# Storing the attention output by head pair, and two loads and a memset moved in the written order

## The chip, the cores and the metric

The kernel runs on one core of one Trainium2 chip. The metric is device time in microseconds of one launch. The core has a matrix engine (TensorE: PE for matmuls, PEld for its weight loads), a vector engine (DVE), a scalar engine (ACT), GpSimd (POOL) and SyncE (SP). SP does no arithmetic here: its instructions wait on semaphores and issue DMAs, one after the other. An instruction that waits on SP holds back everything behind it on SP.

## The reference

Eight batches of eight heads go through block-causal attention (576 tokens, 64 numbers a head, blocks of 64 tokens). The heads of one batch laid side by side are x, 576 rows of 512 floats. Then, for each batch, a score per row is computed, the 128 rows of highest score are picked, and a two-layer network is applied to those rows alone; the other rows are the attention output as it is.

```
scores = (q @ k.T) / 8, masked so that block_i >= block_j
attn   = exp(scores - max) / (sum + 1e-9)
x      = attn @ v, heads side by side            # (8, 576, 512)
s      = x @ w_gate
top    = the 128 rows of highest s, per batch
out    = x
out[top] = x[top] + sigmoid(s[top]) * (relu(x[top] @ w1) @ w2)
```

## The kernel before

**Pairs and beats.** Attention works on pairs of heads: 8 batches of 4 pairs make 32 pairs, p = 0 to 31. What happens to a pair is a list of steps, `STEPS` (lines 52 to 101): each has a time in beats, relative to the beat p of its pair, and a name. The plan (lines 737 to 744) is all steps of all pairs, sorted by p plus that time, and the program is written out in that order. So the order in `STEPS`, modulo one beat, is the order of the instructions on every engine: matmuls for `scores` of pair p are written at the beginning of beat p, those of `times_v` of pair p at p + 2.6857, its `divide` at p + 2.8556. A step is delayed in the plan if what it needs has not been written yet (lines 764 to 783). Every engine runs its own instructions in that order; what it waits for is put in by semaphores on the data.

**What a pair does.** `load` (line 304) brings q and k of the pair, 576 KB in one DMA on SP, into one of three buffers `qk`. `shrink` (line 315) scales q on POOL. `scores` (line 355) is a set of matmuls. `maxima` (DVE) and `exps` (ACT) follow. `turn_p` and `keep_p` transpose the probabilities on PE and copy them out of PSUM. `load_v` (line 324) brings v in two DMAs on SP (264 KB and 99 KB) into one of three buffers `v`, and `ones` (line 332) writes a column of ones into it with one memset on POOL. `times_h` and `times_v` (lines 474 and 492) multiply by v. `invert` and `divide` (lines 510 and 515) divide by the sums and write the pair's 128 columns of `x_sb`, a tile for a whole batch (two of them).

**Which work frees a buffer.** `load` of pair p + 3 writes into the buffer that `scores` of pair p reads, `load_v` of pair p + 3 into the one that `times_v` of pair p reads. In `STEPS`, `load` stands at -2.75, that is 0.25 beats into the beat of the pair whose scores free it; these scores are written at 0.0 to 0.0448. `load_v` stands at 0.05; the `times_v` that frees its buffer stands 0.36 beats earlier (2.6857 - 3 = -0.3143).

**Stores.** At the last pair of a batch `divide` issues four DMAs on SP that store the batch's x (lines 525 to 532): 64 rows, 256 rows and twice 128 rows of 512 floats, 2 KB a row. They wait for the division, the DVE instruction of line 520. In the written order the next `load_v` comes behind them: 0.8556 of one beat against 0.05 of the next.

**Also in SP's queue.** The weights w1 and w2 come in 16 DMAs of 256 KB, behind `scores` of the pairs from the third on (`weights`, line 722). For six batches a row of scores goes out to DRAM and comes back spread over all partitions (`store` and `fetch`, lines 559 and 567). 

**Selection and experts.** When a batch's x is complete, `select` (line 536) makes the steps that rank its rows: five scores on DVE, comparisons on POOL (lines 608 to 620, for all but the last batch), counts by matmul, and row numbers (`idx_all`). They are strewn into later beats at the places that `STEPS` calls `vec`, `far`, `rank` and `spot`. The two-layer network (lines 1013 to 1087) runs behind attention, in two groups of four batches. It gathers its rows from the stored output by an indirect DMA on POOL (line 922), and its first part is begun in the last beats of attention.

Of the kernel before, what the change touches and what calls it, by code (L numbers as in the profile page):

```python
# [18 lines left out]
P = 128  # L19
# [10 lines left out]
PLACES = [1, 3, 0, 2, 4]  # L30
# [20 lines left out]

STEPS = [
    (-2.6704, 'far'),
    (-2.75, 'load'),
    (-0.95, 'shrink'),
    (0.0, 'scores', 2),
    (0.007, 'scores', 1),
# [22 lines left out]
    (0.9042, 'exps', 2),  # L80
    (0.9265, 'keep_p', (8, 7), 0),
    (0.9524, 'vec'),
    (0.05, 'load_v'),
    (0.9954, 'keep_p', (8, 7), 1),
    (1.0825, 'turn_p', (2, 1)),
    (1.108, 'turn_p', (6, 5)),
    (1.1476, 'turn_p', 'h'),
    (1.2343, 'turn_p', (4, 3)),
    (1.1, 'ones'),
    (1.6987, 'keep_p', (6, 5), 0),  # L90
    (1.6996, 'keep_p', (6, 5), 1),
    (1.8986, 'keep_p', (2, 1)),
# [56 lines left out]
def attention_topk_ffn(  # L149
# [11 lines left out]
    nc = tc.nc  # L161
    B, S, _ = out.shape
    H, D = 2 * qk.shape[1], qk.shape[2] // 2
# [33 lines left out]
    for x, r, base in ((0, slice(0, P), 0), (1, slice(0, 64), 64), (1, slice(64, P), 0)):  # L197
        nc.gpsimd.affine_select(
            out=later[x][r], in_=less_b[r], pattern=[[-1, P]], base=base, channel_multiplier=1, compare_op=ALU.is_ge, fill=0.0,
# [32 lines left out]
    def attention(att):  # L232
# [12 lines left out]
        def bank(p, use):  # L245

            return tuple(OTHER[x] for x in BANK[use]) if p % 2 else BANK[use]
# [9 lines left out]
        def give(p, use, part=None):  # L257
            for x in bank(p, use)[slice(None) if part is None else slice(part, part + 1)]:
                assert live[x][0:2] == [p, use], (p, use, live)
                live[x][2] -= 1  # L260
                if not live[x][2]:
                    live[x] = None
# [242 lines left out]
        def outcome(p):  # L505

            at = column(PLACES[0], 0)
            return st[p]["y"][:, at:at + 2 * (NT + 1) * WIDTH].rearrange("p (i h d) -> p i h d", h=2, d=WIDTH)
# [6 lines left out]
        def divide(p):  # L515
            b, h = pairs[p]
            if h == 0:
                xs[b] = xp.tile([P, NT + 1, DM], F32, name="x_sb")
            x = xs[b]
            nc.vector.tensor_tensor(  # L520
                out=x[:, :, h * D:(h + 2) * D].rearrange("p i (h d) -> p i h d", h=2), in0=outcome(p)[:, :, :, 0:D],
                in1=rinvs[p % 2].unsqueeze(3).to_broadcast([P, NT + 1, 2, D]), op=ALU.mult,
            )
            give(p, "y")
            if h == H - 2:
                turned = out[b, 320:S].rearrange("(t x p) d -> x p t d", x=2, p=64)
                nc.sync.dma_start(out=out[b, 0:64], in_=x[64:P, PLACES.index(0), :])
                nc.sync.dma_start(
                    out=out[b, 64:320].rearrange("(t p) d -> p t d", p=P), in_=x[:, PLACES.index(1):PLACES.index(2) + 1:PLACES.index(2) - PLACES.index(1), :],
                )  # L530
                for a in range(2):
                    nc.sync.dma_start(out=turned[1 - a], in_=x[64 * a:64 * a + 64, PLACES.index(3):PLACES.index(4) + 1:PLACES.index(4) - PLACES.index(3), :])
                select(b)
            st[p].clear()

# [156 lines left out]
        def tick(kind, p):  # L692
# [13 lines left out]
        steps = dict(  # L706
            ones=ones, load=load, load_v=load_v, times_h=times_h, invert=invert, shrink=shrink, scores=scores, maxima=maxima, exps=exps,
            turn_p=turn_p, keep_p=keep_p, times_v=times_v, divide=divide,
        )

# [112 lines left out]
        while (N - 1, "divide") not in made:  # L823
# [5 lines left out]
            at, i, p, name, args = plan.pop(n)  # L829
# [293 lines left out]
```

## Time and profile before

| | |
|---|---|
| time, median of 3 runs | 358.36 us (354.39 to 363.0) |
| the profiled execution | 360.99 us, of which the span from first to last instruction is 359.2 us |
| busy: PE / PEld / DVE / ACT / POOL | 338.2 / 279.7 / 256.4 / 239.0 / 194.0 us |
| granted clock of TensorE | 0.999 |
| DMA queue of SP and ACT loads and stores (q1) | 23676 packets, 46.36 MB |
| stores of x | 32 DMAs: 8 of 512 KB, 16 of 256 KB, 8 of 128 KB |

Attention takes the span up to about 259 us, with PE in steps of some 7 us, one beat each; from 252 us on PE has work of the network. "Issue" in a view of waits is time in which an engine waited for nothing that the profile shows. The DMA share of a stretch is the mean busy share of the core's 16 DMA engines; a packet there is one contiguous row moved.

### The profile page before, as it was taken

Reading aid. Unit: us, or ns where it says so; the run is one execution under the profiler, and the core shown is the slowest. Engines: PE = TensorE matmul, PEld = TensorE weight load, DVE = VectorE, ACT = ScalarE, POOL = GpSimd, SP = SyncE. Lnnn points to the kernel's source line nnn. Section 1 sums busy time; section 2 is a strip of 40 time slices with the busy share of each in tenths; the row PEclk is TensorE's granted clock in tenths of the full one; section 3 lists DMA queues with packets and bytes.
Section 4 is the critical chain, followed back from the end, with each engine's and each line's share of the span. In section 5 each row is a group of like instructions: output and inputs, shape, how many; then the busy total and the mean of one; then the engine's idle time right before and its main releaser. Section 6 shows DMA issues by size and latency. Waiting matters only on the chain.

```text
span 359.2 us, 15530 instructions
## 1 busy us (share of the span) xinstructions
PE 338.2 (94%) x6707; PEld 279.7 (78%) x6707; DVE 256.4 (71%) x634; ACT 239.0 (67%) x562; POOL 194.0 (54%) x220
## 2 busy tenths in 40 slices
PE   8899997998899989999989999999999998999993
PEld 4488886887788868888878888789776876888882
DVE  3667886878788977997989899898378497322330
ACT  2899997898799969999989889997172201122000
POOL 2101361087970259989577787918964993310121
PEclk9999999999999999999999999999999999999999
DMA  7565478459556955845763874270040101110001
GB/s 252 175 195 171 147 219 277 144 170 301 160 179 202 297 179 159 267 145 172 228 204 111 256 229 152 84 203 5 2 133 29 29 2 59 58 60 0 29 29 59
DMA packets 25312, 51.83 MB, mean 144 GB/s; under 512 B 6014, under 2 KB 9372, under 8 KB 25244
## 3 DMA queue, kind: packets, MB, share of 16 engines
q1 hardware_dynamic: 23676, 46.36, 41.4%
q0 software_dynamic: 1280, 4.20, 3.5%
q8 instruction: 52, 0.85, 1.0%
q10 hardware_dynamic: 288, 0.30, 0.3%
q14 instruction: 16, 0.13, 0.1%
HBM read 39.29 MB, written 11.55 MB: 142 GB/s over the span
## 4 chain that ended last, share of the span: by engine, by line
PE 67%; POOL 9%; DVE 7%; DMA 6%; issue 4%; ACT 3%; SPq 2%; POOLq 0%; DVEq 0%; ACTq 0%
PE ps L375 21%; PE ps L501 18%; PE ps L439 12%; PE ps L965 6%; PE ps L989 5%; POOL more L618 4%; PE ps L489 3%; ACT p_sb L394 3%; DMA xe<-out_dram,idx_all 2%; DMA v<-in_v_dram 2%; POOL beats1a L620 1%; DVE junk L546 1%; DMA v<-in_vz_dram 1%; PE ps L749 1%; DVE junk_at L643 1%
## 5 line engine op out<-in xcount | busy, mean ns | idle before, releaser
L394 ACT ACTIVATE p_sb<-ps,nmax 128x320 f32<-128x320 f32 (+8 forms) x288 | 130.2, 532 | 14.9 <-DVE nmax L384 7.7
L384 DVE TENSOR_REDUCE nmax<-ps 128x1 f32<-128x320 f32 (+8 forms) x288 | 118.8, 481 | 14.4 <-PE ps L375 14.2
L218 ACT COPY pt<-ps 128x512 f32<-128x512 f32 (+1 forms) x192 | 82.2, 507 | 16.4 <-PE ps L439 15.3
L375 PE MATMUL ps<-qk 64*64 64x64 f32 (+6 forms) x1408 | 88.0, 389 | 1.4 <-issue 0.8
L501 PE MATMUL ps<-v,pt 128*64 128x65 f32 x2560 | 82.3, 222 | 2.3 <-issue 2.2
L501 PEld LDWEIGHTS ps<-v,pt 128*64 128x64 f32 x2560 | 78.4, 137 | 4.7 <-issue 2.8
L439 PE MATMUL ps<-ident,p_sb 64*128 64x64 f32 x1472 | 54.9, 225 | 7.3 <-issue 4.2
L375 PEld LDWEIGHTS ps<-qk 64*64 64x64 f32 x1408 | 49.7, 135 | 14.9 <-issue 7.3
L439 PEld LDWEIGHTS ps<-ident,p_sb 64*128 64x128 f32 x1472 | 49.6, 139 | 11.2 <-issue 6.5
L618 POOL TENSOR_SCALAR more<-sB,sc 64x576 bf16<-64x576 f32 (+6 forms) x47 | 54.2, 1163 | 5.6 <-DMA xe<-out_dram,idx_all 4.1
L989 PE MATMUL ps<-w,h 128*128 128x512 f32 x192 | 45.7, 395 | 0.0
L965 PE MATMUL ps<-xeTh,w 128*128 128x512 f32 x128 | 41.7, 400 | 0.9 <-DVE x_sb L520 0.9
L989 PEld LDWEIGHTS ps<-w,h 128*128 128x128 f32 x192 | 35.8, 188 | 8.0
L322 POOL TENSOR_SCALAR qk<-qk 128x576 f32<-128x576 f32 x31 | 21.7, 699 | 36.0 <-DMA qk<-in_qk_dram 25.2
L971 ACT ACTIVATE h<-ps 128x512 fp32r<-128x512 f32 x16 | 9.6, 598 | 37.8 <-PE ps L965 37.8
L546 DVE CUSTOM_DVE_ANT_0 junk<-x_sb,wg_b 128x512 bf16<-128x512 f32 x40 | 33.2, 829 | 0.1
L999 POOL DMA_INDIRECT out_dram<-y,idx_all x8 | 8.4, 1051 | 44.0 <-DVE y L994 33.8
L489 PEld LDWEIGHTS ps<-v,ph 64*64 64x64 f32 x768 | 21.8, 133 | 12.3 <-issue 10.7
L972 DVE SCALAR_TENSOR_TENSOR h<-ps,h 128x512 fp32r<-128x512 f32 x16 | 11.0, 689 | 27.6 <-ACT h L971 27.6
L965 PEld LDWEIGHTS ps<-xeTh,w 128*128 128x128 f32 x128 | 24.1, 188 | 6.8 <-issue 1.0
L520 DVE TENSOR_TENSOR x_sb<-ps,rinv 128x640 f32<-128x640 f32 x32 | 26.4, 825 | 1.1
L965 PE MATMUL ps<-xeTl,w 128*128 128x512 f32 x64 | 25.4, 396 | 0.0
(71 smaller groups left out, 288.4 us busy)
## 6 DMA issues: line engine op xcount, KB each, us to landing
qk<-in_qk_dram SPq DMA_DIRECT2D x31, 576.0 KB
v<-in_v_dram SPq DMA_DIRECT2D x32, 264.0 KB
w_raw<-in_w_dram SPq DMA_DIRECT2D x16, 256.0 KB
out_dram<-x_sb SPq DMA_DIRECT2D x8, 512.0 KB
out_dram<-x_sb SPq DMA_DIRECT2D x16, 256.0 KB
v<-in_vz_dram SPq DMA_DIRECT2D x32, 99.0 KB
sB<-line SPq DMA_DIRECT2D x6, 192.0 KB
out_dram<-x_sb SPq DMA_DIRECT2D x8, 128.0 KB
```

What stands on the lines that cost most here:

```text
L218: nc.scalar.copy(out=o, in_=i)
L375: nc.tensor.matmul(place(p, t)[64 * o:64 * o + 64, c0:c1], qT[:, 64 * t:64 * t + 64], kT[:, k0:k0 + c1 - c0], start=True, stop=True,)
L384: nc.vector.tensor_reduce(out=s["nmax"][:, c:c + 1], in_=place(p, t), axis=AX.X, op=ALU.max, negate=True)
L394: nc.scalar.activation(out=st[p]["p"][:, first(t):first(t) + ends(t)], in_=place(p, t), func=AF.Exp, bias=st[p]["nmax"][:, c:c + 1], scale ...
L439: nc.tensor.transpose(out=ps[:, a, at], in_=win, identity=ident[r, r])
L489: nc.tensor.matmul(y[64 * c:64 * c + 64, k:k + D + 1], s["ph"][r, a, w], block, start=(z, c) not in begun, stop=False)
L501: nc.tensor.matmul(y[64 * c:64 * c + 64, k:k + D + 1], s["pt"][:, at:at + 64], vt[:, n, hh, 0:D + 1], start=False, stop=hh == 1 and (i, n) ...
L520: nc.vector.tensor_tensor(out=x[:, :, h * D:(h + 2) * D].rearrange("p i (h d) -> p i h d", h=2), in0=outcome(p)[:, :, :, 0:D], in1=rinvs[p ...
L546: nc.vector.tensor_tensor_reduce(out=junk[:, 0:DM], in0=x[:, PLACES.index(t), :], in1=wg_b, scale=1.0, scalar=0.0, op0=ALU.mult, op1=ALU.a ...
L618: eng.tensor_scalar(out=o[r, c:c1], in0=row["sB"][r, c:c1], scalar1=sc[r, t:t + 1], scalar2=None, op0=op)
L965: nc.tensor.matmul(ps[:, 0:ncol], w1_hl[f][:, a, c, :], xeT[g][d][:, c, 0:ncol], start=(c == 0 and t == 0), stop=(c == NC1 - 1 and t == 2),)
L989: nc.tensor.matmul(ps[0:n, 0:DM], h_tile(f)[:, a, begin[g][gi]:begin[g][gi] + n], late["w2"][f][:, d, :], start=(f == 0 and t == 0), stop= ...
```

## The change

The four store DMAs of a batch become four per pair, each of the pair's 128 columns only (512 B a row instead of 2 KB), issued right behind that pair's division. The rows of each of the four stay the same. The bytes stored stay the same; there are 128 store DMAs instead of 32, with 18432 rows of 512 B instead of 4608 of 2 KB.

Three times in `STEPS` change: `load` from -2.75 to -2.95 (0.05 into the beat instead of 0.25), `load_v` from 0.05 to -0.305 (right behind the `times_v` at -0.3143, and ahead of `divide` at -0.1444, that is 2.8556 - 3), and `ones` from 1.1 to 1.0 (ahead of `shrink`, which is at 0.05 of a beat, instead of behind it).

```diff
 STEPS = [
     (-2.6704, 'far'),
-    (-2.75, 'load'),
+    (-2.95, 'load'),
     (-0.95, 'shrink'),
...
-    (0.05, 'load_v'),
+    (-0.305, 'load_v'),
...
-    (1.1, 'ones'),
+    (1.0, 'ones'),
...
             give(p, "y")
+            cols = slice(h * D, (h + 2) * D)
+            turned = out[b, 320:S, cols].rearrange("(t x p) d -> x p t d", x=2, p=64)
+            nc.sync.dma_start(out=out[b, 0:64, cols], in_=x[64:P, PLACES.index(0), cols])
+            nc.sync.dma_start(
+                out=out[b, 64:320, cols].rearrange("(t p) d -> p t d", p=P), in_=x[:, PLACES.index(1):PLACES.index(2) + 1:PLACES.index(2) - PLACES.index(1), cols],
+            )
+            for a in range(2):
+                nc.sync.dma_start(out=turned[1 - a], in_=x[64 * a:64 * a + 64, PLACES.index(3):PLACES.index(4) + 1:PLACES.index(4) - PLACES.index(3), cols])
             if h == H - 2:
-                turned = out[b, 320:S].rearrange("(t x p) d -> x p t d", x=2, p=64)
-                nc.sync.dma_start(out=out[b, 0:64], in_=x[64:P, PLACES.index(0), :])
...
                 select(b)
```

## Rows read from the trace of the kernel before

**Rows 1.** The page: the span, and the engines' busy time with instructions.
```profile
span 359.2 us, 15530 instructions
...
PE 338.2 (94%) x6707; PEld 279.7 (78%) x6707; DVE 256.4 (71%) x634; ACT 239.0 (67%) x562; POOL 194.0 (54%) x220
```

**Rows 2.** Stretches (start:end, length): busy us and instructions by engine, clock, DMA share, GB/s.
```profile
19.67:245.50 225.83, 216.99 (x5844) 187.37 (x5844) 191.96 (x491) 202.54 (x481) 137.18 (x160) 1.00 0.62 190
...
33.78:40.84 7.06, 7.06 (x198) 6.13 (x201) 5.33 (x14) 6.72 (x17) 0.67 (x1) 1.00 0.57 187
...
47.90:56.12 8.22, 7.26 (x198) 6.26 (x201) 6.66 (x18) 6.83 (x17) 2.91 (x5) 1.00 0.84 236
...
117.94:127.67 9.73, 7.42 (x201) 6.35 (x203) 8.50 (x23) 7.16 (x17) 4.42 (x5) 1.00 1.00 302
...
134.93:141.98 7.05, 7.05 (x199) 6.13 (x201) 5.30 (x14) 6.70 (x17) 6.79 (x7) 1.00 0.49 161
...
230.94:238.01 7.07, 7.07 (x199) 6.14 (x195) 6.51 (x17) 6.72 (x18) 3.84 (x5) 1.00 0.76 229
```

**Rows 3.** Waits of PE, 19.67 to 245.5 us: us in total, times, longest.
```profile
PE ps L439 <- issue: 4.2, 3, 2.3
PE ps L501 <- issue: 2.2, 3, 1.2
PE ps L439 <- ACT p_sb L394: 0.9, 1, 0.9
PE ps L375 <- issue: 0.8, 3, 0.5
```

**Rows 4.** Timeline of PE: start, us, instruction, in brackets idle before and its cause.
```profile
54.90 1.22 PE L439 MATMUL ps<-ident,p_sb 64*128 64x64 f32 x32 [0.95 <-issue]
...
85.58 1.64 PE L439 MATMUL ps<-ident,p_sb 64*128 64x64 f32 x45 [0.94 <-ACT p_sb L394]
...
127.40 0.27 PE L439 MATMUL ps<-ident,p_sb 64*128 64x64 f32 x1 [2.31 <-issue]
...
185.39 1.27 PE L439 MATMUL ps<-ident,p_sb 64*128 64x64 f32 x34 [0.92 <-issue]
```

**Rows 5.** The page's DMA queues: packets, MB, share of 16 engines' span.
```profile
q8 instruction: 52, 0.85, 1.0%
q10 hardware_dynamic: 288, 0.30, 0.3%
```

**Rows 6.** Timeline of SP's queue: start, us the issue took, line and DMA.
```profile
39.32 0.33 SPq L329 DMA_DIRECT2D v<-in_v_dram  x1
...
47.66 0.52 SPq L527 DMA_DIRECT2D out_dram<-x_sb  x1
...
48.86 1.47 SPq L532 DMA_DIRECT2D out_dram<-x_sb  x2
...
51.48 1.42 SPq L329 DMA_DIRECT2D v<-in_v_dram  x1
...
238.05 0.40 SPq L329 DMA_DIRECT2D v<-in_v_dram  x1
```

**Rows 7.** Timeline of PE: the work that frees v and qk, two beats.
```profile
43.76 2.55 PE L501 MATMUL ps<-v,pt 128*64 128x65 f32 x80
...
47.83 2.71 PE L375 MATMUL ps<-qk 64*64 64x64 f32 x44
...
233.92 2.55 PE L501 MATMUL ps<-v,pt 128*64 128x65 f32 x80
```

**Rows 8.** Timeline of POOL: memsets of ones that waited for v.
```profile
57.61 0.12 POOL L333 MEMSET v<- 128x14 f32 x1 [6.72 <-DMA v<-in_vz_dram]
...
243.65 0.13 POOL L333 MEMSET v<- 128x14 f32 x1 [4.33 <-DMA v<-in_vz_dram]
```

**Rows 9.** Waits of PE, 245.5 to 309 us.
```profile
PE ps L936 <- DMA xe<-out_dram,idx_all: 1.1, 2, 0.8
```

**Rows 10.** The stretch in which the last batch's stores run alone, columns as in Rows 2.
```profile
260.50:265.50 5.00, 5.00 (x30) 3.80 (x30) 2.90 (x4) 3.13 (x8) 2.95 (x3) 1.00 0.81 239
```

More of the change, by code (lines that the diff above doesn't have):

```diff
@@ L524, in divide @@
             give(p, "y")
-            if h == H - 2:
-                turned = out[b, 320:S].rearrange("(t x p) d -> x p t d", x=2, p=64)
-                nc.sync.dma_start(out=out[b, 0:64], in_=x[64:P, PLACES.index(0), :])
[L528 to L532, printed above, removed]
+            cols = slice(h * D, (h + 2) * D)
[6 more added lines that the diff above has]
+                nc.sync.dma_start(out=turned[1 - a], in_=x[64 * a:64 * a + 64, PLACES.index(3):PLACES.index(4) + 1:PLACES.index(4) - PLACES.index(3), cols])
+            if h == H - 2:
                 select(b)
```

## The prediction

> **What bounds the kernel now.** I read the page first, then the time by stretches, then what PE waits for, and SP's queue last. The page has PE busy 338.2 of 359.2 us [rows 1]: whatever is to be won must come out of the rest. Cut at the starts of successive score blocks, attention is 30 stretches, 19.67 to 245.50 us, and in them PE is idle 225.83 - 216.99 = 8.84 us [rows 2]. A beat without disturbance, the stretch from 33.78, is 7.06 us, all of it PE [rows 2], so no step on DVE, ACT or POOL sets the pace there.
>
> PE's waits in these 30 beats: 4.2 + 2.2 + 0.8 = 7.2 us of "issue" and 0.9 us for the exponentials [rows 3]. "Issue" names no releaser, so I looked at where it falls. Eleven of the 30 stretches have a DMA share of 0.73 or more, the first from 47.90 and the last from 230.94 [rows 2]. Five stops in them, 0.95 at 54.90, the longest, 2.31 at 127.40, and the last, 0.92 at 185.39 among them [rows 4], make 6.3 us; the other 19 stretches share 0.9 us. So 0.57 us per heavy stretch, 0.05 per light one. The stretch with the longest stop has a share of 1.00 [rows 2]. The kernel's code itself comes over the same DMA engines: 52 packets on the instruction queue [rows 5], and 2 x 6707 instructions of PE and PEld [rows 1] over 52 is 258 per packet; a beat has some 399 [rows 2], so PE needs a new packet about every 4.6 us. My reading is that a packet of code comes late where loads and stores crowd the engines. By the Trainium skill, "Runtime: NRT & Kernel Launch", section "Instruction fetch mechanics", crossing a block of code is mostly hidden; if that held here, the 7.2 us would have another cause, and nothing of them would go.
>
> The crowd comes from the batch ends. The stores' four issues last from 47.66 to 48.86 + 1.47 = 50.33; only then comes the v load, at 51.48 [rows 6], with the loads of the next beat on its heels. The multiplication that frees its buffer ended at 43.76 + 2.55 = 46.31 [rows 7]. So v went out 5.2 us late, and POOL's memset waited 6.72 us for v [rows 8]. In a beat without stores v goes out at 39.32 [rows 6], one beat of 7.06 before 46.38, right behind its multiplication.
>
> **The change, part by part.**
>
> Moving `load_v` (two DMAs a pair): in three beats of four it stands where it effectively stood. At the seven batch ends that matter it goes ahead of the stores, 5.2 us earlier. PE did not wait for v itself, so nothing by itself; it takes load out of the pile behind the stores. Moving `load` (one DMA): at 0.25 or 0.05 it waits for the same scores. Behind it on SP stand the weights' DMAs and the fetch of the scores' row, which lose nothing, since they came behind it or the stores before. Nothing. Moving `ones` (one memset of 0.12 us [rows 8]) ahead of `shrink`: if v is late, `shrink` now waits too; its cover is that v is issued one beat of 7.06 us ahead. If that cover went, scores would stop by as much as v is late, 6.72 us at worst [rows 8]; I put nothing.
>
> The stores: 96 more issues. Four issues take SP 2.67 us [rows 6], now in every beat; with v, qk and a weight chunk at 0.33 to 0.52 each, near 4.5 of 7.06 us. An issue can take 1.42 us, as the one at 51.48 did [rows 6], but that was with the engines full, and is then bounded by the DMA work counted next. The four wait for the division, and the next thing behind them that PE needs is qk: the scores that free its buffer end at 47.83 + 2.71 = 50.54 [rows 7], 0.2 us after the last store's issue, so it is not held, and it has two beats in hand. The division of the next pair writes other columns of the same tile; if it waited for the stores to be read, they would have some four us of the beat for that. Nothing.
>
> Rows of 512 B are in no row of this trace. The last batch's 576 rows of 2 KB, alone, took 0.81 x 5.00 = 4.05 us of DMA share [rows 10], 4.05 x 16 / 576 = 112 ns a row. The queue with 288 packets of 1.04 KB took 0.003 x 359.2 x 16 / 288 = 60 ns each [rows 1, 5]. The line through both gives 33 ns at 512 B; the ends are 28 ns (in proportion to 112) and 60 ns (no cheaper than 1 KB). I take 33, being the trend: 576 x 33 / 16 = 1.19 us per pair, against 4.05 / 4 = 1.01 before; the ends are 1.0 and 2.2. On the total that is little. But its place changes: 1.19 / 7.06 = 0.17 on every beat, none at batch ends. A beat without weights, 0.49 in the stretch from 134.93 [rows 2], goes to 0.66; one with a chunk, 0.57 in the stretch from 33.78 [rows 2], to 0.74, and there are about twelve of these (16 chunks, a few beats with two).
>
> The Trainium skill, "DMA: Bandwidth & Descriptors", section "Rules for kernel authors", speaks against this edit: many small transfers should be joined into one large one, and those under 64 KB are mostly overhead; two of a batch's stores were 256 KB and are now 64 KB. By its fit in "Anatomy of one DMA", 2.0 us fixed for each, four in a row would be an estimated 8.7 us and more than a beat. The issues here go out 0.5 to 0.7 us apart and overlap [rows 6], so the sum above stands on the rows' prices.
>
> **The sum.** Issue stops: were all 30 beats light, 30 x 0.05 = 1.5 would be left, and 5.7 be won; were the twelve with weights as bad as heavy ones now, 12 x 0.57 + 18 x 0.05 = 7.7, a loss of 0.5. The twelve reach a share of 0.74 without the pile of loads behind a burst, so I take the middle of 0.05 and 0.57 for them: 12 x 0.31 + 0.9 = 4.6, a gain of 2.6. The 0.9 us for exponentials [rows 3] is one stop, at 85.58 [rows 4], in the beat behind the second batch's end, where the pile is; I let it go: 0.9. After attention, PE waits 1.1 us for gathered rows [rows 9] at the end of a chain of comparisons on POOL that began behind the last memset, 243.65 [rows 8]. Its v load went out at 238.05 [rows 6], though its buffer was free at 233.92 + 2.55 = 236.47 [rows 7]: 1.6 us earlier now, enough for the 1.1. Together 2.6 + 0.9 + 1.1 = 4.6 us. The profiled execution took 360.99 us, 2.6 above the median of the three runs; against the median the sum is 358.4 - 4.6 = 353.8 us.
>
> **The rivals.**
> *All stops go.* Spread evenly, no packet of code is late: 5.7 + 0.9 + 0.5 (the rest of the 8.84 idle) + 1.1 = 8.2, so 350.2. For it: six of the eleven heavy stretches had no issue stop. Against: in the first half, chunks and stores meet.
> *The stops only move.* They belong to how much the engines move, not to when, or have another cause: 7.2 stay; 358 with the chain's 1.1, 357 to 360. For it: stops also fall into lighter stretches (0.9 us).
> *Every beat becomes a heavy one.* Its place is the beat without weights. If a 512 B row costs 47 ns or more (0.73 - 0.49 = 0.24 of 7.06 us, times 16 / 576), the share passes 0.73 in all 30 beats: 30 x 0.57 = 17.1 of stops instead of 7.2, +9.9, so 368. For it: 47 lies between my ends of 28 and 60. Against: the line gives 33.
> *The change doesn't do what it says:* if v still went out behind the stores, the result is that of the stops that only move.
>
> **How the numbers follow.** Forecast 353.8, by itself 351 to 356.5: 0.40. All stops go, 350.2: 0.28. They only move: 0.19. Every beat heavy: 0.13. A median can be told from no change at about 2%, so faster means below 351.2: most of the second case and an edge of the first, 0.30. Slower, above 365.5, is the last case, 0.13; 0.57 lies between. The range of 347.5 to 360.5 takes in the first three, with the floor of the second lowered by the 2.6 us between profile and median, and leaves out the last and little else.
>
> **What would show it.** In SP's queue: every v load within 0.3 us of its multiplication, four stores a beat taking 2.7 us, qk no later than 0.5 us behind the scores. DMA share: no stretch over 0.9, none under 0.55 while attention runs; a store's row of 512 B within 28 to 60 ns. PE's issue in attention near 4.6 us, and mostly in beats with weights. POOL's memsets no longer wait 4 us or more for v. I am wrong if issue stays at 7 us or more with these shares, or if PE waits on qk, v or a division.

## The result, and the profile after

The changed kernel takes 354.32 us in the median of 20 runs (350.73 to 356.32), the kernel before, beside it, 358.71 (354.39 to 363.0): 4.4 us less, where 4.6 were forecast and 353.8 us predicted. The ratio is 0.990, 95% interval 0.9871 to 0.9929: clear of 1, and inside the 2% that the prediction counts as neither faster nor slower. Ratios here leave out runs more than 1.5% above a kernel's fastest; where a kernel's runs spread widely, ratio and median differ, and I give both.

The profiled execution of after took 354.28 us. Its page, first lines and DMA queue, against [rows 1, 5]:

```profile
span 352.6 us, 15629 instructions
...
PE 337.0 (96%) x6707; PEld 279.7 (79%) x6707; DVE 258.4 (73%) x634; ACT 238.7 (68%) x562; POOL 197.9 (56%) x220
...
q1 hardware_dynamic: 39036, 46.37, 44.3%
```

The same queue on the page of before:

```profile
q1 hardware_dynamic: 23676, 46.36, 41.4%
```

PE's work is the same to 1.2 us; the time came out of its idle time. The stretches of after, columns as in [rows 2]; the first is the 30 beats of attention:

```profile
18.93:238.85 219.92, 216.57 (x5849) 188.01 (x5845) 193.26 (x491) 202.31 (x481) 141.93 (x161) 1.00 0.67 197
...
90.60:97.68 7.08, 7.08 (x198) 6.18 (x195) 6.75 (x17) 6.73 (x18) 6.81 (x7) 1.00 0.95 290
...
112.46:120.72 8.26, 7.67 (x196) 6.50 (x196) 7.30 (x21) 6.89 (x17) 2.88 (x5) 1.00 0.88 249
...
217.40:224.65 7.25, 7.25 (x195) 6.34 (x195) 5.38 (x14) 6.66 (x17) 6.99 (x9) 1.00 0.47 117
```

Attention is 225.83 - 219.92 = 5.9 us shorter [rows 2], the way into it 0.7 us, and what follows is as long as it was: 359.2 - 245.50 = 113.7 us before, 352.6 - 238.85 = 113.75 after. That is 6.6 us between two single executions; the one shown of before lay 2.3 us above the median of its 20 runs, so some of it is the draw. PE's waits in attention, against [rows 3]:

```profile
PE ps L375 <- DVE x_sb L520: 1.1, 2, 0.9
PE ps L501 <- issue: 0.5, 1, 0.5
PE ps L375 <- issue: 0.5, 1, 0.5
PE ps L489 <- issue: 0.5, 1, 0.5
```

Issue is 1.5 us instead of 7.2, and the wait for the exponentials is gone. SP's queue and PE around one pair, against [rows 6, 7] (the first line is PE's multiplication that frees v):

```profile
43.07 2.55 PE L501 MATMUL ps<-v,pt 128*64 128x65 f32 x80
```

```profile
45.67 0.33 SPq L329 DMA_DIRECT2D v<-in_v_dram  x1
46.05 0.76 SPq L330 DMA_DIRECT2D v<-in_vz_dram  x1
46.98 0.50 SPq L527 DMA_DIRECT2D out_dram<-x_sb  x1
47.52 0.58 SPq L528 DMA_DIRECT2D out_dram<-x_sb  x1
48.16 1.29 SPq L532 DMA_DIRECT2D out_dram<-x_sb  x2
49.49 0.59 SPq L718 DMA_DIRECT2D w_raw<-in_w_dram  x1
50.19 1.11 SPq L309 DMA_DIRECT2D qk<-in_qk_dram  x1
```

v goes out 0.05 us behind its multiplication (43.07 + 2.55 = 45.62) and ahead of the stores, at a batch end too. But POOL's memset waits for v more than before, not less. Its waits in attention, before and after:

```profile
POOL v L333 <- DMA v<-in_vz_dram: 19.2, 5, 6.7
...
POOL v L333 <- PE ps L631: 10.2, 1, 10.2
...
POOL v L333 <- PE ps L375: 6.6, 3, 4.5
```

```profile
POOL v L333 <- DMA v<-in_vz_dram: 48.3, 9, 8.4
...
POOL v L333 <- PE ps L632: 2.4, 1, 2.4
```

By the first line of each that is 19.2 us before and 48.3 after. Releasers are inferred; all waits of this memset together are 36.0 and 50.7 us.

**Are the issue stops late code?** Two neighbouring stretches of the kernel before, packets by DMA queue: 118.0 to 124.6 us first, then 124.6 to 127.4, which ends with the longest stop (2.31 us, [rows 4]).

```profile
DMA packets 1423, 1.98 MB, mean 300 GB/s; under 512 B 654, under 2 KB 871, under 8 KB 1423
...
q1 hardware_dynamic: 1423, 1.98, 97.7%
```

```profile
DMA packets 333, 0.88 MB, mean 314 GB/s; under 512 B 42, under 2 KB 100, under 8 KB 332
...
q8 instruction: 1, 0.02, 3.0%
```

For 6.6 us, at a share near 1, every packet was data; at PE's need of one code packet in 4.6 us one was due. It came in the next stretch, from 124.75 to 126.08, and PE went on at 127.40. The same holds for every long stop: in the 14 profiles of this study PE has 26 issue stops of 0.8 us or more in attention, and each ended 1.2 to 1.6 us behind the end of a code packet that had begun 5.3 to 9.2 us after the packet before it, where the mean distance in attention is 4.8 to 5.1 us. So the long stops are late code. Some short ones are not: the 0.47 us at 83.07 in after ends 4.0 us behind the last code packet. By the Trainium skill, "Runtime: NRT & Kernel Launch", section "Instruction fetch mechanics", code comes in blocks of 16 KiB and crossing a block is mostly hidden. The trace agrees on the block (0.85 MB in 52 packets); on the hiding it agrees for most of the 52, and not for the five whose lateness PE stopped for, 0.84 to 2.31 us each.

### The profile page after: what moved, and what is told of

Read it like the earlier page. It is cut to its first block, busy times and chain, and to the rows that moved or that the text cites. A ratio compares the mean times of both kernels' runs of the same rounds, so it can differ in the third digit from the quotient of the medians.

```text
span 352.6 us, 15629 instructions
## 1 busy us (share of the span) xinstructions
PE 337.0 (96%) x6707; PEld 279.7 (79%) x6707; DVE 258.4 (73%) x634; ACT 238.7 (68%) x562; POOL 197.9 (56%) x220
## 4 chain that ended last, share of the span: by engine, by line
PE 73%; DVE 12%; POOL 4%; issue 4%; ACT 3%; DMA 3%; POOLq 0%; DVEq 0%; ACTq 0%
PE ps L375 21%; PE ps L501 20%; PE ps L439 12%; PE ps L966 8%; PE ps L990 6%; PE ps L489 3%; DVE nmax L384 3%; DVE junk L547 3%; DMA xe<-out_dram,idx_all 2%; POOL more L619 2%; ACT p_sb L394 2%; DVE junk_at L644 1%; PE ps L750 1%; DVE w L905 1%; DVE x_sb L520 1%
## 5 line engine op out<-in xcount | busy, mean ns | idle before, releaser
L375 PE MATMUL ps<-qk 64*64 64x64 f32 (+6 forms) x1408 | 86.9, 386 | 2.1 <-DVE x_sb L520 1.1
L619 POOL TENSOR_SCALAR more<-sB,sc 64x576 bf16<-64x576 f32 (+6 forms) x47 | 56.2, 1205 | 3.5 <-DMA xe<-out_dram,idx_all 2.0
L547 DVE CUSTOM_DVE_ANT_0 junk<-x_sb,wg_b 128x512 bf16<-128x512 f32 x40 | 34.9, 873 | 0.1
L333 POOL MEMSET v<- 128x14 f32 x32 | 4.0, 124 | 52.0 <-DMA v<-in_vz_dram 49.5
L489 PEld LDWEIGHTS ps<-v,ph 64*64 64x64 f32 x768 | 22.6, 133 | 12.2 <-issue 11.5
```

The lines of the kernel that those rows point to most:

```text
L375: nc.tensor.matmul(place(p, t)[64 * o:64 * o + 64, c0:c1], qT[:, 64 * t:64 * t + 64], kT[:, k0:k0 + c1 - c0], start=True, stop=True,)
L489: nc.tensor.matmul(y[64 * c:64 * c + 64, k:k + D + 1], s["ph"][r, a, w], block, start=(z, c) not in begun, stop=False)
L547: nc.vector.tensor_tensor_reduce(out=junk[:, 0:DM], in0=x[:, PLACES.index(t), :], in1=wg_b, scale=1.0, scalar=0.0, op0=ALU.mult, op1=ALU.a ...
L619: eng.tensor_scalar(out=o[r, c:c1], in0=row["sB"][r, c:c1], scalar1=sc[r, t:t + 1], scalar2=None, op0=op)
```

## The experiments

Theories at first: the **pile** (stops come from a long unbroken run of DMA work behind 1.18 MB of stores), the **order** (what counts is that v leaves ahead of the stores), the **share** (stops follow the mean share, as the forecast priced them). All results together; issue is PE's issue waits in attention, from one profile each. The profiled run lay above its kernel's median by 2.3 us in before, 4.1 in e6_load, 1.3 in e11_ones_back and 1.8 in e12_two_pairs, below it by 1.6 in e4_bunch, 1.8 in e5_v and e10_v_ones and 2.0 in e8_v_behind, and within 0.5 in the rest:

| kernel | v | load | memset | stores | issue, us | median, us (before beside it) | ratio to before, 95% interval |
|---|---|---|---|---|---|---|---|
| before | old | old | old | batch | 7.2 | | |
| after | new | new | new | pair | 1.5 | 354.32 (358.71) | 0.990, 0.9871 to 0.9929 |
| e1_stores | old | old | old | pair | 3.6 | 360.8 (360.27) | 0.999, 0.9945 to 1.0035 |
| e2_order | new | new | new | batch | 1.8 | 354.94 (360.27) | 0.9882, 0.9825 to 0.9938 |
| e3_spread | new | new | new | pair, 8.4 MB more | 6.8 | 361.85 (360.27) | 1.0061, 1.0024 to 1.0099 |
| e4_bunch | new | new | new | pair, 8.4 MB more | 6.8 | 366.08 (360.27) | 1.0158, 1.0109 to 1.0206 |
| e5_v | new | old | old | batch | 2.6 | 357.14 (359.6) | 0.9985, 0.9945 to 1.0025 |
| e6_load | old | new | old | batch | 6.7 | 359.49 (359.6) | 1.0032, 0.9989 to 1.0075 |
| e7_ones | old | old | new | batch | 4.2 | 359.43 (359.6) | 1.0053, 1.0013 to 1.0093 |
| e8_v_behind | old | new | new | pair | 1.0 | 369.14 (359.6) | 1.0311, 1.025 to 1.0373 |
| e9_v_load | new | new | old | batch | 5.7 | 358.92 (358.88) | 0.9841, 0.9761 to 0.9921 |
| e10_v_ones | new | old | new | batch | 2.0 | 355.12 (358.88) | 0.9862, 0.9807 to 0.9918 |
| e11_ones_back | new | new | old | pair | 5.4 | 359.34 (358.88) | 0.9978, 0.9939 to 1.0017 |
| e12_two_pairs | new | new | new | two pairs | 3.7 | 353.91 (358.88) | 0.9818, 0.9766 to 0.9871 |

**The two halves apart.** `e1_stores`: the changed kernel with the old times.

```diff
-    (-2.95, 'load'),
+    (-2.75, 'load'),
-    (-0.305, 'load_v'),
+    (0.05, 'load_v'),
-    (1.0, 'ones'),
+    (1.1, 'ones'),
```

> The stores by pair alone; the three times of the steps as in the kernel before, so v's loads stand behind the four stores of a pair again, now in every beat. Theory of the pile (PE's issue stops come from a long unbroken run of DMA work, made by 1.18 MB of stores with the loads of a beat behind them): the bytes of a burst are cut to a quarter, so most of the gain is here, 355 to 356 us, issue stops in attention under 2.5 us. Rival, the order (what counts is that v leaves ahead of the stores): 357.5 to 359, issue stops of 5 us or more.

Measured 0.999: no gain, though issue fell to 3.6 us. The pile's expectation of 355 to 356 us fails; the rival's time is not far off (360.8 against 359 at most), its issue of 5 or more is not met. In its place PE now waits for other things, the memset of a v that left behind the stores among them:

```profile
PE ps L489 <- POOL v L333: 1.0, 1, 1.0
```

That the time stays is in part the clock, not attention. In this profile 29 beats of attention take 216.54 us (18.23 to 234.77), against 218.41 before (19.60 to 238.01), and what follows takes 124.0 us against 121.2. There PE stood 1.9 us for a score on DVE, where it stood 0.7 before, and right behind it TensorE's granted clock fell to half, 1.2 GHz (the last column but two):

```profile
273.70:277.10 3.40, 3.40 (x10) 2.62 (x9) 0.74 (x3) 0.15 (x1) 2.29 (x3) 0.50 0.43 112
```

So the stores by pair gave nothing in the time; that they gave nothing in attention is not shown.

`e2_order`: the same three lines the other way round, in the kernel before.

> The three times of the steps alone; the stores by batch as before. Theory of the pile: the run of DMA work at a batch's end keeps its 1.18 MB, and only v's 0.36 MB of one beat leaves ahead of it: 357 to 358.5 us, issue stops in attention of 4 us or more. Rival, the order: 354.5 to 356, issue stops under 2.5 us.

Measured 0.9882, issue 1.8 us: the order, as the rival said. The times alone give all that the whole change gives; 1.18 MB still go out in one burst.

**Volume or bunching.** `e3_spread` and `e4_bunch` load 8.4 MB more, that nobody reads, into the changed kernel.

```diff
+    spill = const.tile([P, 4, 512], F32, name="spill")
...
+            z = h // 2                                     # e3_spread: one in every beat
+            nc.sync.dma_start(out=spill[:, z, :], in_=w1[z * P:(z + 1) * P, 0:512])
...
             if h == H - 2:
+                for z in range(4):                         # e4_bunch: four at a batch end
+                    nc.sync.dma_start(out=spill[:, z, :], in_=w1[z * P:(z + 1) * P, 0:512])
```

> The changed kernel with one load more in every beat: 256 KB of w1 into a tile that nobody reads, behind the four stores, 32 x 256 KB = 8.4 MB in all; the result is not touched. At the price of a weight chunk it raises the DMA share of attention from 0.67 by about 0.12. Theory of the pile: the work stays spread, issue stops stay under 3 us, 354 to 356.5 us. Rival, the share (my forecast's 0.57 us of stops for each stretch with a share of 0.73 or more): nearly every beat is over 0.73, stops of 9 to 16 us, 362 to 369 us.

> The changed kernel with the same 8.4 MB more, but bunched: four loads of 256 KB behind the stores of each batch's last pair, none in the other beats. Theory of the pile: a run of 1.05 MB at each batch's end brings the stops back, 4 to 8 us, 357 to 361 us, at least 2 us more than the same bytes spread. Rival, the share: as with the bytes spread or better, since three beats of four stay under 0.73.

Spread, the bytes cost 7.5 us against after's 354.32, by medians of different sessions (6.0, if each is first taken against the before beside it), and issue goes from 1.5 to 6.8 us: the pile's 354 to 356.5 fails, and the share's 362 to 369 is missed by little, with less issue than the 9 to 16 expected. Bunched they cost 4.2 us more than spread, at the same issue; the difference came from other waits, of which this is the longest (ranks that wait for POOL's comparisons):

```profile
PE ps L635 <- POOL beats1a L608: 2.3, 1, 2.3
```

So both count: how much is moved, and that it is bunched, each by a part.

**The three times apart.** One line each in the kernel before, and v put back alone in the changed one.

```diff
-    (0.05, 'load_v'),
+    (-0.305, 'load_v'),      # e5_v
-    (-2.75, 'load'),
+    (-2.95, 'load'),         # e6_load
-    (1.1, 'ones'),
+    (1.0, 'ones'),           # e7_ones
...
-    (-0.305, 'load_v'),      # e8_v_behind, in the changed kernel
+    (0.05, 'load_v'),
```

> The kernel before with one step moved: load_v ahead of the division, so ahead of the batch's stores. Theory V (the gain of the order is v leaving before the stores; at a batch end the run of loads behind the stores is shorter by v's 363 KB): a ratio of 0.988 to 0.993, issue stops in attention 2 to 3 us. Theory Q (qk stood behind v and the stores, and its being earlier is the gain): 0.997 to 1.002. Theory P (the memset's place on POOL is the gain): 0.997 to 1.002.

> The kernel before with load alone moved, so that the qk load stands ahead of the v load of its beat; both still behind the batch's stores. Theory V: 0.997 to 1.002, issue stops of 5 us or more. Theory Q: 0.988 to 0.993. Theory P: 0.997 to 1.002.

> The kernel before with the memset alone moved, ahead of shrink on POOL. SP's queue is untouched. Theories V and Q: 0.998 to 1.003. Theory P: 0.988 to 0.993.

> The changed kernel with load_v alone put back to 0.05, behind the four stores of a pair. Theory V: most of the gain is lost again, a ratio of 0.997 or more to the kernel before. Theories Q and P: the gain stays, 0.987 to 0.993.

None of the three gains by itself beyond its interval: Q and P fail as sole causes, and V by the ratio, 0.9985. By the medians v alone gives 0.993 (357.14 against 359.6), over half of the gain, so a part of its own is not excluded. The memset alone is 0.5% slower by the ratio and no different by the medians. And v put behind the stores, with the memset ahead of `shrink`, costs 3.1%: the loss that V expected, and far more than that. Most of it is seen in its trace. POOL's waits in attention, and PE's:

```profile
POOL v L333 <- DMA v<-in_vz_dram: 45.6, 12, 11.8
POOL v L333 <- PE ps L375: 32.8, 5, 11.4
```

```profile
PE ps L632 <- POOL beats1a L605: 6.8, 2, 4.2
PE ps L632 <- POOL beats0a L605: 2.3, 1, 2.3
PE ps L375 <- issue: 1.0, 4, 0.3
```

POOL stands at the memset for 78 us, for a v that leaves late (the second line names PE's scores, but the memset's tile is v; releasers are inferred). Behind the memset stand `shrink` and the comparisons of the selection; their sums are late, and PE, which counts them in order, stands 9.1 us in three stops, of 2.34, 4.21 and 2.64 us. In each of them or right behind it TensorE's granted clock fell to half, 1.2 GHz. Below are the longest such stretch and the three sets of 80 multiplications by v behind the stops; such a set took 2.55 us in the kernel before [rows 7]:

```profile
151.40:158.20 6.80, 4.84 (x84) 4.71 (x85) 1.54 (x5) 0.90 (x2) 6.62 (x9) 0.50 0.28 108
```

```profile
110.90 3.88 PE L501 MATMUL ps<-v,pt 128*64 128x65 f32 x80
...
153.56 4.59 PE L501 MATMUL ps<-v,pt 128*64 128x65 f32 x80
...
216.17 4.10 PE L501 MATMUL ps<-v,pt 128*64 128x65 f32 x80
```

That is 1.3 + 2.0 + 1.6 = 4.9 us more, so the stops cost some 14 us with what the clock adds; the median lies 14.8 us above after's 354.32. The granted clock was 0.977 to 0.983 in all six runs, and 0.995 or more in the 20 of after. Issue is the lowest of all, 1.0 us: a kernel with hardly an issue stop can be the slowest.

**Which pairs of them.** `e9_v_load` and `e10_v_ones` are the kernel before with two of the lines above; `e11_ones_back` is the changed kernel with the memset's line back at 1.1.

> The kernel before with load_v and load moved, the memset in its old place, stores by batch. With v alone the ratio was 0.9985, with all three times 0.9882. Theory L (v and qk must both leave at once, and SP must not hold either): 0.986 to 0.992, issue stops in attention under 2.5 us. Theory M (v early pays only with the memset ahead of shrink on POOL): 0.995 to 1.000, issue stops of 2.5 us or more.

> The kernel before with load_v and the memset moved, load in its old place, stores by batch. Theory L: 0.995 to 1.000. Theory M: 0.986 to 0.992, issue stops under 2.5 us.

> The changed kernel with the memset alone put back to 1.1, behind shrink. Theory L: the gain stays, 0.986 to 0.993. Theory M: it goes, 0.996 to 1.001. In both, POOL waits less for v than the 48.3 us of the changed kernel in attention.

v with the memset gains the whole (0.9862), as theory M said and L did not. With the memset back, the changed kernel loses its gain (0.9978, issue 5.4 us): M again. `e9_v_load` doesn't decide. Its six runs go from 353.15 to 360.93, the ratio rests on the two lowest (0.9841, on L's side), the median is that of before, and the profile, of a run of 358.69 us, has 5.7 us of issue. M stands by two of the three. What the memset's place changes on POOL is seen in `e11_ones_back` and `e10_v_ones`. POOL's waits in attention, first with the memset behind `shrink`:

```profile
POOL qk L322 <- DMA qk<-in_qk_dram: 15.1, 4, 5.9
...
POOL v L333 <- DMA v<-in_vz_dram: 4.4, 3, 2.8
```

```profile
POOL v L333 <- DMA v<-in_vz_dram: 59.4, 11, 9.8
POOL w L896 <- DMA w_raw<-in_w_dram: 13.9, 2, 7.1
```

Behind `shrink`, the memset waits until qk, 576 KB, has landed, and in `e11_ones_back` PE once waits for it:

```profile
PE ps L489 <- POOL v L333: 1.7, 1, 1.7
```

Ahead of it, POOL waits for v, nearly 60 us in all, and PE does not wait for POOL. That accounts for 1.7 us of e11's loss. Its longest issue stop, 3.03 us, waited for code too, a packet that began 9.2 us after the one before it; behind that stop, which ended at 130.90, the granted clock was at half from 132.1 to 135.5. Why issue is higher too with the memset behind (5.4 and 5.7 us against 2.0, 1.8 and 1.5) is not settled: SP's order is the same, and no run separates it from the draw of one profile each.

**A coarser store.** `e12_two_pairs` stores every second pair, rows of 1 KB.

```diff
-            cols = slice(h * D, (h + 2) * D)
...
+            if h % 4 == 2:
+                cols = slice((h - 2) * D, (h + 2) * D)
...
```

> The changed kernel with the stores issued for two pairs at a time: rows of 1 KB, 64 store DMAs instead of 128, each half as late on the mean as by batch. The stores by pair (0.990) and by batch with the new order (0.9882) came out alike, so if the stores' grain doesn't matter this is 0.986 to 0.993 too. If the burst still counts for something and the 512 B rows as well, this is the best of the three, 0.980 to 0.986.

Measured 0.9818, 353.91 us, the lowest median of the study. It beats the kernel before; against the changed kernel, 354.32 in another session, it isn't told apart: the two intervals meet at 0.9871. So the expectation that burst and 512 B rows both count, 0.980 to 0.986, is met by the ratio and not decided. By the Trainium skill, "DMA: Bandwidth & Descriptors", section "Rules for kernel authors", small transfers should be joined and those under 64 KB are mostly overhead. With the new order, transfers of 32 to 128 KB (0.990), 64 to 256 KB (0.9818) and 128 to 512 KB (0.9882) were not clearly told apart; no run here shows that overhead in the time.

## Why the prediction was right, step by step

The time, the sign and the kind of saving were right: less issue on PE in attention, PE's work unchanged. Several steps under it were not, and they made up for each other: that 353.8 came within 0.6 us of the median, 354.32, is luck.

- **v leaves behind its multiplication, ahead of the stores: right** for 22 of the 29 loads that wait for a buffer, which go out within 0.1 us of it; six miss the 0.3 us that the prediction allowed, and the latest goes out 1.58 us behind. Before, v was 4.1 to 5.7 us late at the seven batch ends, and 1.3 to 4.0 in five of the beats behind them, which the prediction took for undisturbed. That the move is worth "nothing by itself" holds in `e5_v` by the ratio, 0.9985, and not by the medians; that the gain is carried by the spread of the stores does not hold. This is the step that failed most: the stores by pair alone give nothing in the time (`e1_stores`), the order alone gives everything (`e2_order`, `e10_v_ones`).
- **The memset, put at nothing: wrong.** Named was its risk, that `shrink` waits if v is late; `e8_v_behind` shows that risk at 3.1%, through the comparisons behind the memset rather than through the scores, as I had it. Not seen was its use: with v early it is needed for the gain (`e11_ones_back`). Nor do POOL's waits for v go away, as forecast; they grow from 36.0 to 50.7 us, the longest now 8.4, and PE does not wait for them.
- **The issue stops, 7.2 to 4.6 us: right in direction, the term mis-sized;** 1.5 us in the profile of after. Twelve stretches have a share of 0.73 or more, as forecast, but they hold 0.9 us of stops, 0.08 each, where the sum charged 0.31, a middle that no row had given. The price by share was poor: the stretch from 90.60 has 0.95 and no stop. Nor does a late code packet always stop PE: in that stretch one began at 93.49, 6.1 us after the one before it. What else it takes is not shown. Still, `e3_spread` brought 6.8 us back by volume, so the rival in which every beat becomes heavy was a real one; it was the 512 B row that was cheap enough.
- **The 512 B row, 33 ns: right.** q1's busy share is 0.443 x 352.6 = 156.2 us against 0.414 x 359.2 = 148.7 before: 7.5 us for 32 pairs, 0.23 us a pair where 0.18 was worked out. The 18462 packets of 512 B in after took 33 ns on the mean. By the Trainium skill, "DMA: Bandwidth & Descriptors", section "Anatomy of one DMA", the fit of 2.0 us from which the prediction had an estimated 8.7 us is the one for DMAs that GpSimd issues; these stores are issued by SP, and four in a row hold it for 2.5 us above (46.98 to 49.45). The share of attention went from 0.62 to 0.67. But it is less even than forecast: 0.95 at most and 0.38 at least, where I had "none over 0.9, none under 0.55".
- **The 0.9 us for exponentials: right**, gone, though perhaps for another reason: that stop, too, ended 1.2 us behind a code packet (83.39 to 84.35) that had begun 6.4 us after the one before it. In their place 0.6 us more go to a division's bank (0.5 us before).
- **The 1.1 us behind attention: wrong.** The stretch is as long as before. POOL's chain did begin earlier, its last memset stands at 234.66 (first line below), 4.2 us ahead of the end of the 30 beats at 238.85, where it was 1.9 us ahead before (243.65 [rows 8], 245.50). PE waits 1.2 us for the gathered rows all the same (second). The chain of waits of after, in order of time, runs through DVE on its way there (third fence), and DVE's work there is what it was. That DVE alone sets this end was not tried.

```profile
234.66 0.13 POOL L333 MEMSET v<- 128x14 f32 x1 [6.07 <-DMA v<-in_vz_dram]
```

```profile
PE ps L937 <- DMA xe<-out_dram,idx_all: 1.2, 2, 0.9
```

```profile
264.22 1.10 DVE junk L547
265.36 0.69 DVE junk L547
266.06 0.60 DVE w L905
266.67 0.60 DVE h L973
267.27 0.45 DVE junk_at L644 x2
```

- **Among the rivals**, "all stops go" at 350.2 was near in issue and not in time: 1.5 us were left as it said, but the rest of its sum (the 0.5 of idle, the 1.1) did not come.

## What to carry to other kernels

In an in-order queue, put each load right behind the work that frees its buffer and ahead of stores that wait for later work; then look at the consumer's queue as well, since the small step that waits for that load holds all that stands behind it, and here the two orders paid in full only together. Undo a change of several lines one line at a time before naming its cause: here the line that looked like the change (the stores) gave nothing in the time. Look at the granted clock beside the waits, since a stop can cost more than its own length. And where PE stops for "issue", count the packets on the instruction queue in that stretch beside the DMA share.

## What the runs showed of the hardware

- PE stopped up to 2.31 us, and in one experiment 3.03 us, for code that came late: in attention all 26 issue stops of 0.8 us or more ended 1.2 to 1.6 us behind the end of a code packet. Before the one of 2.31 us, a stretch of 6.6 us held 1423 data packets and no code packet.
- TensorE's granted clock fell to half, 1.2 GHz, in or right behind PE stops of 1.9 us in `e1_stores`, 2.0 in `e3_spread`, 3.0 in `e11_ones_back` and 2.3 to 4.2 in `e8_v_behind`, where 80 multiplications then took 3.9 to 4.6 us instead of 2.55. Behind the 2.31 us of before it did not fall.
- A store in rows of 512 B instead of 2 KB, four times the packets, took 0.23 us more DMA time a pair, 23% more.
- An issue on SP took 0.33 to 0.6 us in most of the lines above, and 1.11 us in the qk load at 50.19. The DMA share in that 1.1 us was 0.63, so full DMA engines do not explain it alone.
